# Sixteen block products in place of eighteen: a Strassen-like scheme for the second pair's up-projections

## The chip, the cores and the metric

The kernel runs on one core of one Trainium2 chip. The core has a matrix engine, TensorE (PE in the profile, its weight loads PEld), and three engines for everything between the products: VectorE (DVE), ScalarE (ACT) and GpSimd (POOL). SyncE (SP) issues the DMA transfers here, all of them on its one queue. Each engine works through its own list of instructions in order; between engines there are only semaphores. Products land in PSUM, in which the kernel uses eight banks of 128 x 512 floats; everything else lies in SBUF.

The metric is the device time of one run in microseconds. Before the change it is 773.49 us, the median of three runs (773.17 to 774.0).

## The reference, cut to what matters

```python
def _attn_ref(q, k, v, alpha):          # 4 x 8 heads, 768 steps, 48 wide
    for t in range(S):
        state = alpha[:, :, t, :, None] * state + np.einsum('bhd,bhe->bhde', k[:, :, t], v[:, :, t])
        y[:, :, t] = np.einsum('bhd,bhde->bhe', q[:, :, t], state)

def _moe_ref(x, w_in, w_out):           # 3072 x 384, w_in 384 x 2048
    h = x @ w_in
    return (h * np.cos(h)) @ w_out

def _moe2_ref(x, w1, w2, w3, w_out):    # w1, w2, w3 384 x 768, w_out 768 x 384
    h = np.maximum(np.maximum(x @ w1, x @ w2), x @ w3)
    return h @ w_out

def reference(q, k, v, alpha, moe_*, moe2_*):
    x = attn_out as 3072 rows of 384
    return _moe2_ref(_moe_ref(x, ...), ...)
```

The change concerns the three up-projections x @ w1, x @ w2 and x @ w3 of the last function.

## The kernel before

The 3072 tokens are cut into six units of 512 (HB). Features lie along the partitions, tokens along the free dimension, so a 384-wide vector is three blocks (NR) of 128. Every matrix product works on a 128 x 128 weight block and a 128 x 512 token block, and is made three times: both operands are split into a high part in TensorE's fast float format and a low remainder, and high x high, high x low and low x high are added up in PSUM. So one "block product" is three matmul instructions.

There are two stages. In the first, attention for a unit (functions turn and visit, in small matmuls) runs between the steps of the first pair of matrices: moe1, one step for each of 16 hidden blocks of 128 (NF1), 96 steps in all. A step takes three block products up (lines 665 to 667), then q, cosine and product on ACT and DVE (lines 673 to 677), the split into gh and gl (678, 679), and three block products down into the three accumulators acc (696 to 698). At the end of a unit ACT and DVE split the three accumulators into a high and a low part (lines 705, 706) and SP stores both in DRAM as x1d.

The second stage is moe2_h and moe2_o. For each unit u and each of six hidden blocks f (NF2), moe2_h takes nine block products: three weights m by three input blocks cc, lines 747 to 749, each weight into a PSUM bank of its own. ACT copies the first bank to t, DVE takes the maximum with the second (755) and the third (757), ACT and DVE split the result into h (758, 759). moe2_o multiplies h by w_out (770 to 772), ACT copies the result to y (775) and SP stores it (776). The function x2_in reads a unit's x1d back (732). The nine blocks w0h to w2l of each f are made by the function weight: the host's float64 numbers come in by DMA (line 363), ACT and DVE turn them into float32 (364, 365), ACT takes the high part (369) and POOL the remainder (373). For the second stage that happens 18 times for w1 to w3, due in steps 78 to 90 of the first stage, and six times for w_out.

The order of all of this is worked out before the program is written. Each piece of work is recorded by op with an engine, a cost, the names that it reads and writes, and a due time in steps. Program.order then plays the list through, engine by engine, taking among what is ready the piece with the smallest due time, and the instructions are written in that order; it also chooses the PSUM bank for each result (five banks ps, and the three acc). On the chip the order within an engine is fixed, and the semaphores decide when each instruction starts. A cost or a due time in the table therefore changes only the order. The flag port in op keeps a piece of POOL's work and a marked piece of DVE's apart in that plan; the written program has no semaphore for it.

Of the kernel before, what the change touches and what calls it, by code (L numbers as in the profile page):

```python
# [47 lines left out]
NWB = NW1 + 3 * NF2 + NF2  # L48
INV2PI = 1.0 / (2.0 * math.pi)
TWOPI = 2.0 * math.pi  # L50


# [4 lines left out]
LIMIT = {"h": 3, "a": 3, "t": 2, "w": 1, "r": 2, "y": 2, "r0": 2, "s0": 2}  # L57
# [184 lines left out]
def dve(n):  # L242
    return 0.07 + 0.00104 * n
# [37 lines left out]
def tile_kernel(ctx, tc, aa, qk, vv, wt, outT):  # L281
# [6 lines left out]
    x1d = dram.tile([NU, NR, P, 2, HB], F32, name="x1d")  # L288
# [17 lines left out]
    gh_b = [mp.tile([P, HB], F32R, name=f"gh{i}") for i in range(NG)]  # L306
    gl_b = [mp.tile([P, HB], F32R, name=f"gl{i}") for i in range(NG)]
    yy_b = [mp.tile([P, 2, HB], F32R, name=f"yy{i}") for i in range(2)]
# [24 lines left out]
    g_b = [ap.tile([PR, AL], F32, name=f"g{i}") for i in range(NGS)]  # L333

# [59 lines left out]
    def att0(k, p, t0):  # L394
# [7 lines left out]
        if k == 3:  # L402
            v, vk = v_b[2], ("v", 2)
            t, na = inv_b[0], "iv0"
            al_to = inv_f[0]
            gf, kg = inv_b[1][:, 0:AL], ("iv1",)
            kq_to = yy_b[1].bitcast(F32).rearrange("p a b -> p (a b)")
            kq_, kk_ = kq_to[0:PR], "yy1"
# [248 lines left out]
    def moe1(i):  # L657
# [34 lines left out]
        for c in range(NR):  # L692
# [7 lines left out]
            op("PE", 3 * mm(HB, P), omm, [("gh", gn), ("gl", gn), ("woh", f), ("wol", f)], [("acc", c)], i + 1.5)  # L700
        if f == NF1 - 1:
            for c in range(NR):
                yn = 1
                o, k = yy_b[yn], f"yy{yn}"
                op("Act", act(HB, True), lambda c=c, o=o: se.activation(o[:, 0], acc[c], AF.Copy), [("acc", c)], [(k, "h"), *((x, k) for x in ("ink", "inq") if not i // NF1)], i)
# [6 lines left out]

    def open_w2():
        s_at.close()
        wp2 = ctx.enter_context(tc.tile_pool(name="w2p", bufs=1))
        for n in "hl":
            w2t[n] = [wp2.tile([P, NF2, NR, P], F32R, name=f"w{m}{n}") for m in range(3)]

    def open_np():
        s_w1.close()  # L720
        np_ = ctx.enter_context(tc.tile_pool(name="np", bufs=1, side="right"))
        w2t["h2"] = [np_.tile([P, NF2, 2, HB], F32R, name=f"h2_{i}") for i in range(2)]
        w2t["t"] = [np_.tile([P, HB], F32, name=f"t2_{i}") for i in range(2)]
        w2t["y"] = [np_.tile([P, HB], F32, name=f"y2_{i}") for i in range(2)]
# [4 lines left out]
    def x2_in(u, t0):  # L729
        n = u % 2  # L730
        for c in range(NR):
            op("SP", HW, lambda c=c: nc.sync.dma_start(x_tile(NU + u).bitcast(F32)[:, c], x1d[u, c]),
               [("x1d", u, c)] + ([("xtA", n)] if c else []),
               [*halves(n, c), ("xp", n, c, 0), ("xp", n, c, 1)] + ([] if c else [("xtA", n)]), t0, dma(P * HB * 8))

    def moe2_h(u, f, t0):
        xn, hn, qn = u % 2, u % 2, (u * NF2 + f) % 2

        def t():
            return w2t["t"][qn]  # L740

        for m in range(3):
            k, ps = psum("a")
            for cc in range(NR):
                def hmm(cc=cc, m=m, ps=ps):
                    xt = x_tile(NU + u)
                    pe.matmul(ps, w2t["h"][m][:, f, cc], xt[:, cc, 0], start=(cc == 0), stop=False)  # L747
                    pe.matmul(ps, w2t["h"][m][:, f, cc], xt[:, cc, 1], start=False, stop=False)  # L748
                    pe.matmul(ps, w2t["l"][m][:, f, cc], xt[:, cc, 0], start=False, stop=(cc == NR - 1))  # L749

                op("PE", 3 * mm2(HB, P), hmm, [*halves(xn, cc), ("xtA", xn), ("w2h", m, f), ("w2l", m, f)], [k], t0 + 0.3 * m)
            if m == 0:
# [237 lines left out]
```

## Time and profile before

| | |
|---|---|
| Median of three runs | 773.49 us (773.17 to 774.0) |
| Span of the profiled execution | 772.1 us |
| PE busy | 762.7 us (99%), 5863 matmuls |
| DVE, ACT, POOL busy | 431.2 us (56%), 348.7 us (45%), 126.0 us (16%) |
| TensorE clock granted | 1.00 of full speed throughout |
| DMA | 72.21 MB, mean 94 GB/s |

The median of the runs is 1.4 us above the span of the profiled execution: the runs are timed from outside the program's first and last instruction. PE's matmuls overlap, since each starts before the one ahead of it has ended, so a busy PE row says that PE never waits, not that it does more in a microsecond than it can. For the other engines a row gives the time from an instruction's start to its end; two instructions that do not depend on each other may overlap by about a tenth of a microsecond. The window rows give busy microseconds of each engine in a stretch. An instruction's line in the profile is its line in the kernel before.

### The profile page before, as it was taken

Reading aid. Unit: us, or ns where it says so; the run is one execution under the profiler, and the core shown is the slowest. Engines: PE = TensorE matmul, PEld = TensorE weight load, DVE = VectorE, ACT = ScalarE, POOL = GpSimd, SP = SyncE. Lnnn points to the kernel's source line nnn. Section 1 sums busy time; section 2 is a strip of 40 time slices with the busy share of each in tenths; the row PEclk is TensorE's granted clock in tenths of the full one; section 3 lists DMA queues with packets and bytes.
Section 4 is the critical chain, followed back from the end, with each engine's and each line's share of the span. In section 5 each row is a group of like instructions: output and inputs, shape, how many; then the busy total and the mean of one; then the engine's idle time right before and its main releaser. Section 6 shows DMA issues by size and latency. Waiting matters only on the chain.

```text
span 772.1 us, 14185 instructions
## 1 busy us (share of the span) xinstructions
PE 762.7 (99%) x5863; PEld 626.8 (81%) x5863; DVE 431.2 (56%) x720; ACT 348.7 (45%) x669; POOL 126.0 (16%) x133
## 2 busy tenths in 40 slices
PE   8999999999999999999999999999999999999998
PEld 6677788888888888888888888888888888888886
DVE  8899998687856776765557654432221312213121
ACT  5788756455555655465568754411121211111121
POOL 5655431120310221110023301100000000000000
PEclk9999999999999999999999999999999999999999
DMA  9777633232312231121027504220020200200001
GB/s 342 261 234 237 187 114 108 59 105 80 118 55 60 92 116 47 45 94 36 8 82 271 167 20 139 88 81 28 14 96 28 82 27 14 96 25 4 22 19 42
DMA packets 27232, 72.21 MB, mean 94 GB/s; under 512 B 3392, under 2 KB 6464, under 8 KB 27168
## 3 DMA queue, kind: packets, MB, share of 16 engines
q1 hardware_dynamic: 27168, 71.31, 27.7%
q8 instruction: 46, 0.75, 0.4%
q14 instruction: 18, 0.15, 0.1%
HBM read 55.17 MB, written 14.16 MB: 90 GB/s over the span
## 4 chain that ended last, share of the span: by engine, by line
PE 88%; DVE 1%; ACT 1%; issue 0%; DVEq 0%; ACTq 0%
PE ps L749 10%; PE ps L748 10%; PE ps L747 9%; PE acc L696 8%; PE acc L698 8%; PE ps L665 8%; PE acc L697 8%; PE ps L667 7%; PE ps L666 7%; PE ps L771 3%; PE ps L772 3%; PE ps L770 3%; PE ps L563 1%; PE ps L581 1%; PE ps L588 1%; PE ps L537 1%
## 5 line engine op out<-in xcount | busy, mean ns | idle before, releaser
L665 PE MATMUL ps<-xt,wih 128*128 128x512 f32 x288 | 115.1, 400 | 0.4 <-ACT woh L369 0.4
L696 PE MATMUL acc<-gh,woh 128*128 128x512 f32 x288 | 114.0, 396 | 0.2 <-ACT gh L686 0.2
L698 PE MATMUL acc<-gl,woh 128*128 128x512 f32 x288 | 112.5, 391 | 0.4 <-DVE gl L691 0.4
L666 PE MATMUL ps<-xt,wih 128*128 128x512 f32 x288 | 112.3, 390 | 0.4 <-DVE xt L501 0.4
L667 PE MATMUL ps<-xt,wil 128*128 128x512 f32 x288 | 112.4, 390 | 0.0
L697 PE MATMUL acc<-gh,wol 128*128 128x512 f32 x288 | 112.2, 390 | 0.0
L674 DVE SCALAR_TENSOR_TENSOR q<-q,ps 128x512 f32<-128x512 int32 x96 | 65.4, 681 | 48.4 <-ACT q L673 48.2
L757 DVE TENSOR_TENSOR ps<-t,ps 128x512 f32<-128x512 f32 x36 | 25.1, 696 | 106.7 <-PE ps L749 106.7
L673 ACT ACTIVATE q<-ps 128x512 int32<-128x512 f32 x96 | 57.2, 595 | 57.5 <-PE ps L667 55.8
L675 ACT ACTIVATE q<-q 128x512 f32<-128x512 f32 x96 | 60.5, 631 | 43.4 <-DVE q L674 42.6
L679 DVE TENSOR_TENSOR gl<-q,gh 128x512 fp32r<-128x512 f32 x80 | 57.8, 724 | 32.9 <-ACT gh L678 30.4
L758 ACT ACTIVATE h<-ps 128x512 fp32r<-128x512 f32 x36 | 21.6, 600 | 113.4 <-DVE ps L757 113.4
L677 DVE TENSOR_TENSOR q<-q,ps 128x512 f32<-128x512 f32 x80 | 54.7, 684 | 27.5 <-ACT q L675 26.5
L678 ACT ACTIVATE gh<-q 128x512 fp32r<-128x512 f32 x80 | 50.2, 629 | 35.1 <-DVE q L677 31.9
L698 PEld LDWEIGHTS acc<-gl,woh 128*128 128x128 f32 x288 | 54.0, 188 | 13.0 <-DVE gl L691 1.3
L755 DVE TENSOR_TENSOR t<-t,ps 128x512 f32<-128x512 f32 x36 | 24.8, 688 | 71.3 <-PE ps L749 71.2
L665 PEld LDWEIGHTS ps<-xt,wih 128*128 128x128 f32 x288 | 54.1, 188 | 12.2 <-ACT woh L369 0.8
L696 PEld LDWEIGHTS acc<-gh,woh 128*128 128x128 f32 x288 | 54.0, 188 | 11.9 <-ACT gh L686 0.6
L667 PEld LDWEIGHTS ps<-xt,wil 128*128 128x128 f32 x288 | 54.1, 188 | 11.8 <-POOL wil L373 0.4
L666 PEld LDWEIGHTS ps<-xt,wih 128*128 128x128 f32 x288 | 54.1, 188 | 11.4 <-DVE xt L501 0.8
L697 PEld LDWEIGHTS acc<-gh,wol 128*128 128x128 f32 x288 | 54.1, 188 | 10.6
L775 ACT ACTIVATE y<-ps 128x512 f32<-128x512 f32 x18 | 10.8, 600 | 93.2 <-PE ps L772 93.2
(147 smaller groups left out, 1452.4 us busy)
## 6 DMA issues: line engine op xcount, KB each, us to landing
raw<-in_wt SPq DMA_DIRECT2D x56, 384.0 KB, 3.9
kq<-in_qk SPq DMA_DIRECT2D x23, 512.0 KB, 4.2
x1d<-yy SPq DMA_DIRECT2D x18, 512.0 KB, 2.7
xt<-x1d SPq DMA_DIRECT2D x18, 512.0 KB, 4.7
al<-in_aa SPq DMA_DIRECT2D x23, 261.0 KB, 2.8
outT<-y SPq DMA_DIRECT2D x18, 256.0 KB, 2.0
v<-in_vv SPq DMA_DIRECT2D x23, 192.0 KB, 4.6
xt<-yy SPq DMA_DIRECT2D x30, 64.0 KB, 3.3
```

The lines of the kernel that those rows point to most:

```text
L665: pe.matmul(ps, wi["h"][:, f, cc], xt[:, cc, 0], start=(cc == 0), stop=False)
L666: pe.matmul(ps, wi["h"][:, f, cc], xt[:, cc, 1], start=False, stop=False)
L667: pe.matmul(ps, wi["l"][:, f, cc], xt[:, cc, 0], start=False, stop=(cc == NR - 1))
L674: op("DVE", dve(HB), lambda: ve.scalar_tensor_tensor(q, q.bitcast(I32), -TWOPI, ps, ALU.mult, ALU.add), [hk], [qk], m)
L675: op("Act", act(HB), lambda: se.activation(q, q, AF.Sin, bias=0.5 * math.pi), (), [qk], m)
L679: op("DVE", dve(HB), lambda: ve.tensor_tensor(gl, q, gh.bitcast(F32), ALU.subtract), [qk, ("gh", gn)], [("gl", gn)], m, port=True)
L696: pe.matmul(acc[c], oh, gh, start=(f == 0), stop=False)
L697: pe.matmul(acc[c], ol, gh, start=False, stop=False)
L698: pe.matmul(acc[c], oh, gl, start=False, stop=(f == NF1 - 1))
L747: pe.matmul(ps, w2t["h"][m][:, f, cc], xt[:, cc, 0], start=(cc == 0), stop=False)
L748: pe.matmul(ps, w2t["h"][m][:, f, cc], xt[:, cc, 1], start=False, stop=False)
L749: pe.matmul(ps, w2t["l"][m][:, f, cc], xt[:, cc, 0], start=False, stop=(cc == NR - 1))
```

## The change

For one hidden block f and two units the kernel before computes 3 weights x 2 units x 3 input blocks = 18 block products. The changed kernel computes the same six results with 16, by a scheme of Strassen's kind: some of the products take a sum or difference of token blocks and a sum or difference of weight blocks, and the results are put together from the products by additions. There are 12 forms of token blocks for each pair of units (A_FORMS) and 16 forms of weight blocks for each f (B_FORMS). The work on one f for one pair of units is called a cell; there are 3 pairs x 6 f = 18 cells.

- **b_prep** makes the 16 weight forms, for three f at a time (a group g, two groups), during the first stage, from step 22 on and 2.6 steps apart for each of 18 weight blocks. A block is loaded and made into float32 as before (ACT, DVE), POOL makes the sums (comb), ACT and POOL split each form (split), and SP stores it in DRAM as bfd.
- **b_load** reads the 16 forms of a cell back, in two halves of 8 forms (1 MB each), into one of two buffers bs_0 and bs_1. The second buffer lies where the first stage's weights were.
- The end of a unit stores the plain accumulator (x1r, a copy by ACT) in place of a high and a low part. **a_prep** reads six such blocks for a pair, makes seven sums on POOL and splits the 12 forms on ACT and DVE: for the first pair in steps 79 to 95, for the others around the down-projections of the pair before.
- **cell** makes the 16 products, five copies of products to SBUF by ACT, one sum by POOL, and the differences and maxima on DVE; finish adds the last part in PSUM and splits h.
- **down** is moe2_o for one unit of a pair, now in one piece behind the pair's six cells; it was spread between the up-projections of the next unit.

gh and gl become the two halves of one tile gg, and the kernel is built with dynamic_dma_scratch_size=1024, which leaves more SBUF for tiles.

```diff
 
-NWB = NW1 + 3 * NF2 + NF2
+NG2 = 2
+NB2 = 9 * NG2
+WO2 = NW1 + NB2
...
+B_ORDER = ((0, 2), (1, 2), (0, 1), (0, 0), (1, 0), (2, 0), (2, 1), (2, 2), (1, 1))
+B_FORMS = ("14", "g1", "22", "21", "6", "23", "13", "8", "10", "15", "7", "11", "2", "9", "12", "32")
+A_FORMS = ("S14", "S1", "a22", "T", "P", "Q", "a11", "a21", "S10", "a13", "a23", "S7")
+NBW, NAS, NH2 = 7, 12, 12
+B_START, B_STEP = 22, 2.6
...
-                op("DVE", dve(HB), lambda c=c, o=o: ve.tensor_tensor(
-                    o[:, 1], acc[c], o.bitcast(F32)[:, 0], ALU.subtract), [("acc", c), (k, "h")], [(k, "l")], i)
-                op("SP", HW, lambda c=c, o=o: nc.sync.dma_start(x1d[u, c], o.bitcast(F32)), [(k, "h"), (k, "l")], [("x1d", u, c)], i, dma(P * HB * 8))
+                op("SP", HW, lambda c=c, o=o: nc.sync.dma_start(x1r[u, c], o), [k], [("x1r", u, c)], i, dma(P * HB * 4))
...
+    def b_prep(g, first, gate):
...
+        def load(j, buf):
...
+                op("Act", act(WB) + 0.1, lambda: se.activation(upper, head, AF.Copy), [rk], [("top", 0)], t)
+                op("DVE", dve(WB), lambda: ve.scalar_tensor_tensor(o.bitcast(U32), x, 13, top, ALU.logical_shift_right, ALU.bitwise_or), [("top", 0), rk], [("bw", buf)], t, port=True)
...
+        def comb(to, x, y, sub=True):
+            op("Pool", pool(WB), lambda: ge.tensor_tensor(bw_b[to], bw_b[x], bw_b[y], ALU.subtract if sub else ALU.add), [("bw", x), ("bw", y)], [("bw", to)], n[0] + 0.1)
+
+        def split(name, buf):
...
+            op("Act", act(WB), lambda: se.activation(st[:, :, 0], x, AF.Copy), [("bw", buf)], [("bs", m, 0)], n[0] + 0.2)
+            op("Pool", pool(WB), lambda: ge.tensor_tensor(st[:, :, 1], x, st.bitcast(F32)[:, :, 0], ALU.subtract), [("bw", buf), ("bs", m, 0)], [("bs", m, 1)], n[0] + 0.2)
+            op("SP", HW, lambda: nc.sync.dma_start(bfd[3 * g:3 * g + 3, :, i].rearrange("f p h n -> p f h n"), st.bitcast(F32)),
+               [("bs", m, 0), ("bs", m, 1)], [("bfd", g, i)], n[0] + 0.3, dma(P * WB * 8))
...
+    def a_prep(p, t0, dt, gate=None):
...
+    def b_load(ci, t0):
+        f, x = ci % NF2, ci % 2
+        for h in range(2):
+            hs = slice(NBF // 2 * h, NBF // 2 * (h + 1))
+            op("SP", HW, lambda hs=hs: nc.sync.dma_start(w2t[f"bs{x}"].bitcast(F32)[:, hs], bfd[f, :, hs]),
+               [("bfd", f // 3, i) for i in range(hs.start, hs.stop)] + ["w2", *(["np"] if x else [])], [("Bs", x, h)], t0 + 1.33 * h, dma(P * NBF * P * 4))
...
+    def cell(p, f, t0):
...
+                pe.matmul(bank, bt[:, i, 0], at[:, 0], start=start, stop=False, skip_group_check=skip)
+                pe.matmul(bank, bt[:, i, 0], at[:, 1], start=False, stop=False, skip_group_check=skip)
+                pe.matmul(bank, bt[:, i, 1], at[:, 0], start=False, stop=stop, skip_group_check=skip)
...
+        product(d21, k21, "S14", "14", True, True)
+        copy("14", d21, k21)
+        product(d23, k23, "S1", "g1", True, True)
+        copy("1", d23, k23)
+        both("u", "14", "1", ALU.add)
+        k12, d12 = psum("m")
+        product(d12, k12, "a22", "22", True, True)
+        copy("22", d12, k12)
+        k11, d11 = psum("m")
+        product(d11, k11, "T", "21", True, True)
+        copy("12", d11, k11)
+        product(d12, k12, "P", "6", False, True)
+        join("s1", d12, k12, "u", ALU.subtract, True)
+        k13, d13 = psum("m")
+        product(d13, k13, "Q", "23", True, True)
+        copy("16", d13, k13)
+        product(d11, k11, "a11", "13", False, True)
+        join("s1", d11, k11, "s1", ALU.max)
+        product(d21, k21, "a21", "8", False, False)
+        product(d21, k21, "S10", "10", False, True)
+        join("s2", d21, k21, "12", ALU.subtract)
+        both("s2", "s2", "22", ALU.max)
+        product(d13, k13, "a13", "15", False, True)
+        join("s1", d13, k13, "s1", ALU.max)
+        r1k, r1 = psum("m")
+        product(r1, r1k, "a11", "7", True, True)
+        product(r1, r1k, "a13", "11", False, True)
+        finish(0, r1, r1k, "s1")
+        product(d23, k23, "a23", "2", False, False)
+        product(d23, k23, "S7", "9", False, True)
+        join("v", d23, k23, "16", ALU.subtract)
+        both("s2", "s2", "v", ALU.max)
+        r2k, r2 = psum("m")
+        product(r2, r2k, "a21", "12", True, True)
+        product(r2, r2k, "a23", "32", False, True)
+        finish(1, r2, r2k, "s2")
...
+        for g in range(NG2):
+            b_prep(g, first, lambda j: B_START + B_STEP * j)
...
+        a_prep(0, NS - 17, 1.1, NS - 17)
+        b_load(0, NS - 6)
...
+        b_load(1, NS + 0.5)
...
+                cell(p, f, t)
...
+                    b_load(n, t + 1.33)
...
+                a_prep(p + 1, t - CB, 0.2)
```

Where the order changes, three places show how. The rows name line, operation and tiles (result, arrow, operands, with the numbers of their buffers); the lines of the changed kernel are its own.

The first is TensorE in the up-projections of the second stage, before: xt6 holds a unit's tokens, w1h to w2l are high and low parts of weights, ps4 and ps1 two PSUM banks.

```order
L747 MATMUL ps4_103<-xt6_4328,w1h_4229 128x512
L748 MATMUL ps4_103<-xt6_4328,w1h_4229 128x512
L749 MATMUL ps4_103<-xt6_4328,w1l_4232 128x512
L747 MATMUL ps1_100<-xt6_4328,w2h_4230 128x512
L748 MATMUL ps1_100<-xt6_4328,w2h_4230 128x512
L749 MATMUL ps1_100<-xt6_4328,w2l_4233 128x512
```

In the changed kernel, the third to the sixth product of a cell: as2 to as5 are token forms, bs_1 is a buffer of weight forms.

```order
L907 MATMUL ps1_99<-as2_4400,bs_1_4978 128x512
L908 MATMUL ps1_99<-as2_4400,bs_1_4978 128x512
L909 MATMUL ps1_99<-as2_4400,bs_1_4978 128x512
L907 MATMUL ps3_101<-as3_4401,bs_1_4978 128x512
L908 MATMUL ps3_101<-as3_4401,bs_1_4978 128x512
L909 MATMUL ps3_101<-as3_4401,bs_1_4978 128x512
L907 MATMUL ps4_102<-as5_4403,bs_1_4978 128x512
L908 MATMUL ps4_102<-as5_4403,bs_1_4978 128x512
L909 MATMUL ps4_102<-as5_4403,bs_1_4978 128x512
L907 MATMUL ps1_99<-as4_4402,bs_1_4978 128x512
L908 MATMUL ps1_99<-as4_4402,bs_1_4978 128x512
L909 MATMUL ps1_99<-as4_4402,bs_1_4978 128x512
```

A bank of before is filled by nine matmuls in a row and read afterwards; in a cell the sixth product adds to ps1, which the third has filled and which ACT copies in between, with two products of other banks behind the third.

The second is ACT in the second stage, before: t2 is the first of the three maxima's operands, h2 the high part of the result.

```order
L753 ACTIVATE t2_0_4845<-ps4_103 128x512
L758 ACTIVATE h2_1_4844<-ps0_99 128x512
L753 ACTIVATE t2_1_4846<-ps2_101 128x512
L758 ACTIVATE h2_1_4844<-ps4_103 128x512
L753 ACTIVATE t2_0_4845<-ps1_100 128x512
```

And one cell of the changed kernel, with the high part h2_5 of the cell before it: q and xf hold the copied products.

```order
L915 ACTIVATE q_83<-acc0_95 128x512
L915 ACTIVATE q_83<-acc1_96 128x512
L932 ACTIVATE h2_5_4984<-ps0_98 128x512
L915 ACTIVATE q_83<-ps1_99 128x512
L915 ACTIVATE xf_4931<-ps3_101 128x512
L915 ACTIVATE xf_4931<-ps4_102 128x512
L932 ACTIVATE h2_6_4985<-ps2_100 128x512
```

The copy of ps1, for which the sixth product waits, stands behind the last result of the cell before.

The third is POOL in the first stage, before: kq holds keys and queries of the attention, g and al its decay factors, d a state.

```order
L527 TENSOR_TENSOR kq0_104<-kq0_104,al0_124 112x512
L642 TENSOR_TENSOR d0_112<-s3_118,g2_129 112x192
L524 TENSOR_TENSOR kq1_105<-kq1_105,g1_128 112x512
L527 TENSOR_TENSOR kq1_105<-kq1_105,al1_125 112x512
L642 TENSOR_TENSOR d0_112<-s0_115,g0_127 112x192
```

At the same place of the changed kernel (its attention buffers have other numbers), bw are weight blocks and sums of them, bs their split forms:

```order
L539 TENSOR_TENSOR kq0_103<-kq0_103,al0_123 112x512
L786 TENSOR_TENSOR bw0_129<-bw0_129,bw2_131 128x384
L794 TENSOR_TENSOR bs0_136<-bw2_131,bs0_136 128x3x128
L794 TENSOR_TENSOR bs1_137<-bw0_129,bs1_137 128x3x128
L654 TENSOR_TENSOR d0_111<-s3_117,g2_128 112x192
L786 TENSOR_TENSOR bw4_133<-bw3_132,bw2_131 128x384
L786 TENSOR_TENSOR bw3_132<-bw3_132,bw1_130 128x384
L786 TENSOR_TENSOR bw2_131<-bw2_131,bw1_130 128x384
L794 TENSOR_TENSOR bs0_136<-bw4_133,bs0_136 128x3x128
L794 TENSOR_TENSOR bs1_137<-bw3_132,bs1_137 128x3x128
L536 TENSOR_TENSOR kq1_104<-kq1_104,g1_127 112x512
L539 TENSOR_TENSOR kq1_104<-kq1_104,al1_124 112x512
```

Between two multiplications of the attention there now stand eight pieces of the weight forms, and the d of before is among them.

## Rows read from the trace of the kernel before

**Rows 1.** Windows: stretch, length, busy us and instructions by engine, clock, DMA.
```profile
80.00:100.00 20.00, 19.39 (x240) 15.16 (x232) 18.76 (x36) 13.94 (x30) 9.38 (x11) 1.00 0.52 160
100.00:134.00 34.00, 34.00 (x455) 28.03 (x453) 30.56 (x53) 20.50 (x41) 7.68 (x7) 1.00 0.39 125
134.00:354.00 220.00, 220.00 (x2429) 181.95 (x2421) 158.25 (x266) 121.01 (x233) 38.84 (x36) 1.00 0.24 79
354.00:480.00 126.00, 126.00 (x748) 104.03 (x739) 74.66 (x120) 76.21 (x141) 22.03 (x22) 1.00 0.32 102
480.00:768.00 288.00, 288.00 (x1272) 238.36 (x1270) 77.32 (x112) 56.73 (x96) 4.48 (x5) 1.00 0.13 46
```

**Rows 2.** Timeline of PE (start us, us, engine, line, operation, tiles).
```profile
470.26 0.39 PE L747 MATMUL ps<-xt,w0h 128*128 128x512 f32 x1
...
480.46 0.39 PE L747 MATMUL ps<-xt,w0h 128*128 128x512 f32 x1
```

**Rows 3.** Groups by line: count, busy us, mean ns, idle before.
```profile
L747 PE MATMUL ps<-xt,w0h 128*128 128x512 f32 x108 | 42.0, 389 | 0.0
```

**Rows 4.** Windows of line 696 alone (PE busy and count).
```profile
0.00:134.00 134.00, 23.05 (x57) 10.70 (x57) 1.00 0.65 214
134.00:354.00 220.00, 55.57 (x141) 26.46 (x141) 1.00 0.24 79
```

**Rows 5.** Groups by line, other engines.
```profile
L364 ACT ACTIVATE top<-raw 128x384 f16<-128x384 bf16 x56 | 35.6, 640 | 2.3 <-DMA raw<-in_wt 1.9
L524 POOL TENSOR_TENSOR kq<-kq,g 112x512 f32<-112x512 f32 x20 | 26.7, 1333 | 58.3 <-DMA kq<-in_qk 29.0 <-DVE g L521 12.4 <-DVE inv L523 7.5
...
L365 DVE SCALAR_TENSOR_TENSOR raw<-raw,top 128x384 uint32<-128x384 uint32 x40 | 25.4, 635 | 3.4 <-ACT top L364 2.0 <-issue 1.2
...
L373 POOL TENSOR_TENSOR wil<-raw,wih 128x384 fp32r<-128x384 f32 x16 | 16.8, 1052 | 20.2 <-ACT wih L369 17.7 <-DVE inv L431 1.8 <-POOL kq L649 0.5
...
L369 ACT ACTIVATE w1h<-raw 128x384 fp32r<-128x384 f32 x6 | 3.3, 550 | 2.0 <-DVE raw L365 2.0
```

**Rows 6.** Line 677 by itself: ns min/median/max, first and last start.
```profile
L677 DVE TENSOR_TENSOR q<-q,ps x80: 652/689/691, 111.3 to 472.5; 128x512 f32<-128x512 f32 x80
```

**Rows 7.** Line 679 by itself, in the same form.
```profile
L679 DVE TENSOR_TENSOR gl<-q,gh x80: 649/692/1646, 113.8 to 473.9; 128x512 fp32r<-128x512 f32 x80
```

**Rows 8.** Timeline, 400 to 404 us, DVE and POOL.
```profile
400.06 0.56 DVE L365 SCALAR_TENSOR_TENSOR raw<-raw,top 128x384 uint32<-128x384 uint32 x1 [0.37 <-ACT top L364]
...
402.18 1.04 POOL L373 TENSOR_TENSOR w0l<-raw,w0h 128x384 fp32r<-128x384 f32 x1 [4.25 <-ACT w0h L369]
...
402.73 0.90 DVE L365 SCALAR_TENSOR_TENSOR raw<-raw,top 128x384 uint32<-128x384 uint32 x1 [0.36 <-ACT top L364]
```

**Rows 9.** Timeline, 84.8 to 87.2 us, ACT, PE and DVE.
```profile
84.84 0.59 ACT L686 ACTIVATE gh<-ps 128x512 fp32r<-128x512 f32 x1
...
85.31 0.61 ACT L673 ACTIVATE q<-ps 128x512 int32<-128x512 f32 x1
...
85.48 0.50 PE L696 MATMUL acc<-gh,woh 128*128 128x512 f32 x1 [0.18 <-ACT gh L686]
...
85.82 0.40 PE L697 MATMUL acc<-gh,wol 128*128 128x512 f32 x1
85.91 0.68 DVE L691 TENSOR_TENSOR gl<-ps,gh 128x512 fp32r<-128x512 f32 x1
...
86.51 0.68 DVE L674 SCALAR_TENSOR_TENSOR q<-q,ps 128x512 f32<-128x512 int32 x1
```

**Rows 10.** Timeline at 560 us: issues on SP's queue.
```profile
560.21 1.28 SPq L732 DMA_DIRECT2D xt<-x1d  x3
```

**Rows 11.** DMA issues by line: KB each, median us to landing.
```profile
xt<-x1d SPq DMA_DIRECT2D x18, 512.0 KB, 4.7
```

**Rows 12.** Timeline of POOL at 251 us.
```profile
251.37 1.20 POOL L527 TENSOR_TENSOR kq<-kq,al 112x512 f32<-112x512 f32 x1
```

**Rows 13.** Timeline of PE at 276 us.
```profile
276.70 0.69 PE L563 MATMUL ps<-kq 48*64 48x64 f32 x32
```

More of the change, by code (lines that the diff above doesn't have):

```diff
@@ L56 @@
 NBANK = 5
[L57 removed]
+LIMIT = {"h": 3, "m": 4, "t": 2, "w": 1, "r": 2, "y": 2, "r0": 2, "s0": 2}
 GLE1, GLQ = 0, 16
@@ L333, in tile_kernel @@
     g_b = [ap.tile([PR, AL], F32, name=f"g{i}") for i in range(NGS)]
+    bw_b = [ap.tile([P, WB], F32, name=f"bw{i}") for i in range(NBW)]
+    bs_b = [ap.tile([P, 3, 2, P], F32R, name=f"bs{i}") for i in range(2)]
     chosen = {}
@@ new lines, in a_prep, with due, step, comb @@
+    def a_prep(p, t0, dt, gate=None):
+        ar = lambda i: w2t["ar"][i]
+        R = {f"a{i + 1}{k + 1}": 3 * i + k for i in range(2) for k in range(NR)}
+        m = [0]
+        def due():
+            return t0 + dt * m[0]
+        def step():
+            return [("step", int(gate + dt * m[0]))] if gate else []
+        for x in ("a12", "a22", "a11", "a13", "a23", "a21"):
+            i = R[x]
+            op("SP", HW, lambda i=i: nc.sync.dma_start(ar(i), x1r[2 * p + i // 3, i % 3]), [("x1r", 2 * p + i // 3, i % 3), "w2"], [("ar", i)], t0 - 2, dma(P * HB * 4), tiled=True)
+        def comb(to, x, y, sub=False):
+            op("Pool", pool(HB), lambda: ge.tensor_tensor(ar(to), ar(x), ar(y), ALU.subtract if sub else ALU.add), [("ar", x), ("ar", y), *step()], [("ar", to)], due())
+        def split(name, i):
+            n = A_FORMS.index(name)
+            o = lambda: a_slot(n)
+            hk, lk = ("as", n, 0), ("as", n, 1)
+            extra = x_freed(0) if n == 9 and not p else []
+            need = [("xtA", 0)] if n in (10, 11) and not p else []
+            op("Act", act(HB), lambda: se.activation(o()[:, 0], ar(i), AF.Copy), [("ar", i), "w2", *need, *step()], [hk, *extra], due())
+            op("DVE", dve(HB), lambda: ve.tensor_tensor(o()[:, 1], ar(i), o().bitcast(F32)[:, 0], ALU.subtract), [("ar", i), hk], [lk], due(), port=True)
+            m[0] += 1
+        comb(6, R["a12"], R["a22"])
+        comb(7, R["a11"], R["a12"])
+        split("Q", 7)
+        comb(R["a12"], R["a12"], R["a13"], True)
+        split("P", 6)
+        comb(7, R["a12"], R["a22"])
+        split("S14", 7)
+        comb(6, 6, R["a11"])
+        split("S1", 6)
+        split("a22", R["a22"])
+        split("T", R["a12"])
+        comb(7, 7, R["a23"], True)
+        split("a11", R["a11"])
+        split("a21", R["a21"])
+        split("S10", 7)
+        comb(6, 6, R["a21"])
+        split("a13", R["a13"])
+        split("a23", R["a23"])
+        split("S7", 6)
@@ L882, in build @@
-        for c in range(NR):
-            moe2_o(NU - 1, c, NS + 2 + NB * NU + c)
+            weight(WO2 + f, lambda f=f: w2t["oh"][:, f], lambda f=f: w2t["ol"][:, f],
+                   ("w2oh", f), ("w2ol", f), NS + 8 + f, ["np"])
+        CB = 16 / 6
+        PB = NF2 * CB + 6
+        for p in range(NU // 2):
+            t0 = NS + 2 + PB * p
+            for f in range(NF2):
+                t = t0 + CB * f
+                cell(p, f, t)
+                n = NF2 * p + f + 2
+                if n < NF2 * NU // 2:
+                    b_load(n, t + 1.33)
+            t = t0 + CB * NF2
+            if p + 1 < NU // 2:
+                a_prep(p + 1, t - CB, 0.2)
+            for i in range(2):
+                for c in range(NR):
+                    down(p, i, c, t + 3 * i + c)
@@ L969 @@
     w1 = _np.stack([blocks(inputs["moe_w_in"], rows), outs(inputs["moe_w_out"])], 1).reshape(-1, P, WB)
-    w2 = _np.stack([blocks(inputs["moe2_" + n]) for n in ("w1", "w2", "w3")], 1).reshape(-1, P, WB)
+    ws = [_np.asarray(inputs["moe2_" + n]) for n in ("w1", "w2", "w3")]
+    w2 = _np.stack([ws[m][k * P:(k + 1) * P, g * WB:(g + 1) * WB] for g in range(NG2) for k, m in B_ORDER])
     wt = _np.ascontiguousarray(_np.concatenate([w1, w2, outs(inputs["moe2_w_out"])]))
```

212 lines of the change are left out of this document (138 added, 74 removed).

## The prediction

> **What bounds the kernel now.** I read the windows first, then the stretch in which the changed code runs. From 100 us on PE is busy in every microsecond of every window: 34.00 of 34.00, 220.00 of 220.00, 126.00 of 126.00, 288.00 of 288.00; between 80 and 100 us it lacks 0.61 [rows 1]. The clock column is 1.00, so all of this is at the upper level, 2.4 GHz. In the second stage, from 480 us, DVE is busy 77.3 of 288 us, ACT 56.7, POOL 4.5, and DMA 0.13 of its time: PE alone sets the end, and the others have three quarters of their time free. Then comes the price of one matmul. A group's row gives 389 ns for it [rows 3], but matmuls overlap. From the one at 470.26 to the one 45 places later at 480.46 [rows 2] it is 10.20 / 45 = 0.2267 us from start to start, and that is what one more or one less is worth.
>
> **The matmuls removed.** A hidden block of two units took 18 block products, 54 matmuls, and takes 16, 48. The trace has 108 matmuls for each of nine kinds (three weights, three lines; one of the nine is in [rows 3]), 972 in all; 18 cells x 48 are 864. 108 x 0.2267 = 24.5 us less on the engine that sets the end. The 324 down matmuls stay, in blocks of 108 behind each pair. Whether the 24.5 us are kept depends on what PE has to wait for, so each addition is held against PE's time.
>
> **Weight forms, in the first stage.** Line 696 has 57 matmuls before 134 us and 141 from there to 354 us [rows 4]; three make a step, so this stretch holds steps 19 to 65. b_prep, from step 22 on with its first load gated on step 19, lies in it almost whole. Before, the 18 weight blocks of w1 to w3 were made later, around 400 us [rows 8]. Added here: 18 x 0.64 and 32 x 0.55 us on ACT, 18 x 0.635 on DVE, 24 sums and 32 remainders at about 1.05 on POOL [rows 5]. That is 29, 11 and 59 us, which makes ACT 150, DVE 170 and POOL 98 of 220 us. None of these is full.
>
> DVE and POOL disturb each other, though. The same instruction of line 365 took 0.56 us at 400.06 with POOL idle and 0.90 at 402.73 beside POOL's of 402.18 [rows 8]. Line 679, with both operands in SBUF, ranges to 1.646 us over a median of 0.692 [rows 7]; line 677, with one operand in PSUM, stays between 0.652 and 0.691 [rows 6]. If each of POOL's 56 pieces costs DVE 0.34 us, DVE is at 189 of 220 us, 86%. From 100 to 134 us it was at 30.56 of 34, 90%, and PE waited for nothing; from 80 to 100 us it was at 94% and PE lacked 0.61 us. The bounds are therefore 0 and 0.61 x 11 = 6.7 us; less than nothing is excluded, since PE has no idle time here to give back. I take 0.5, near the row with the like load. What hides the work is that a step gives PE four microseconds and that its chain on ACT and DVE runs ahead of PE; where that cover is gone, each late gl holds PE, and all of PE's queue behind it.
>
> The Trainium skill has a rule that speaks against this edit ("SBUF — State Buffer", section "Who interferes with whom"): a DVE instruction with two SBUF inputs contends with a GpSimd instruction that reads SBUF, for one port pair that is locked for a whole instruction. This trace agrees: line 679 suffers and line 677 does not. By that rule alone each of the 56 pieces can block DVE for its whole length, and the sum would be that of the second rival below.
>
> SP's queue gets 32 stores that wait for POOL's remainders, with loads for the attention behind them. Those have room: POOL's product of 251.37 [rows 12] is used by PE's matmuls from 276.70 on [rows 13], 24 us later. Cost 0; once the room is gone, a visit of the attention would wait on PE.
>
> **Token forms.** A pair costs 12 copies on ACT, 12 subtractions on DVE and 7 sums on POOL, at about 0.60, 0.69 and 1.33 us [rows 9, 7, 5]: 7, 8 and 9 us. The first pair's fall in steps 79 to 95, from which the 18 weight blocks have gone; DVE was at 74.7 of 126 us there with them [rows 1]. The others fall beside 108 down matmuls, 24.5 us. Cost 0. The 18 subtractions at the units' ends leave DVE, for which PE did not wait: gain 0.
>
> **The cell.** Sixteen products take 16 x 0.680 = 10.88 us. DVE has 11 pieces of 0.69, 7.6 us; ACT 7 of 0.60, 4.2; POOL one of 1.33. What matters is the chain. Product k (from 0) starts 0.68 k after the cell and can be read at 0.68 k + 0.84 (two pitches and 0.389); an engine is taken to start 0.04 after that, an estimate. The narrow place is the sixth product, due at 3.40, whose bank ACT has to copy first; ACT's queue ahead of that copy holds the high part of the previous cell's last result. In that cell DVE takes product 9 at 7.00 (a maximum), then the maximum in SBUF, the sum with product 11 at 8.36 to 9.05; ACT's high part ends at 9.69, DVE's low part starts at 9.72, v at 10.32, the next maximum at 11.05, the last sum at 11.77 to 12.46, which is 1.58 in the new cell. The steps of 0.60 and not 0.68 between instructions that do not depend on each other are those of DVE's two starts at 85.91 and 86.51; ACT's are 0.47 at 84.84 and 85.31 [rows 9]. ACT then copies product 1 at 1.56, the high part at 2.03, the third product at 2.50 to 3.10. With no overlap at all DVE ends at 1.87 and that copy at 3.40. PE goes on 0.16 us after ACT: gh ended at 85.43, the second matmul behind it started at 85.82, so the first went at 85.59 [rows 9]. The sixth product can thus go at 3.26, before its turn, or at 3.56, 0.16 late. The bounds are 0 and 0.16 us in each of the 15 cells that follow a cell, 0 and 2.4 us; I take 0.3, since the rows show the overlap. Next narrowest is the second product: v has read its bank at 11.01, and it is due at 11.56.
>
> **Weight forms read back.** Each cell reads 2 x 1.05 MB, of which it has 10.88 us: 193 GB/s. Three loads of 512 KB were issued within 1.28 us [rows 10] and took 4.7 us to land [rows 11], so 1.57 MB in at most 6.0 us, 262 GB/s: 8.0 us for a cell. Taken as one at a time, 0.52 MB in 4.7 us are 112 GB/s and 18.8 us for a cell. I take the first, as the rows describe loads side by side, and cost 0. The second buffer's first load can only go when the first stage's last product is done; 12 products, 8.2 us, then stand ahead of the second cell, and half a buffer needs 4.0 to 6.0.
>
> **The sum.** 772.1 - 24.5 + 0.5 + 0.3 = 748.4 us of span; the last copy and store are as before. The runs lie 1.4 us above the span, so 749.8 us for the median, 23.7 less, 3.1%.
>
> **The rivals.**
> - *The cell's chain is the longer one.* 0.16 us late in 15 cells: 749.8 - 0.3 + 2.4 = 751.9; at twice that, 754.3. For it: a slack of a tenth of a microsecond. Against it: DVE has 3 us of each cell free, so a late cell does not add up with the next.
> - *DVE and POOL lock each other in the first stage.* If each of 56 pieces costs DVE 0.95 us, the excess of the longest in [rows 7], DVE is wanted for 223 of 220 us and stops hiding; with 0.34 of each then on PE it is 749.3 + 19 = 768. It decides from about 95% of DVE in that stretch. Against it: PE's idle 0.00 at 90%.
> - *The weight forms come late (slower).* If a cell's loads take 18.8 us, PE waits 7.9 us at 16 cells, 126 us: 876. It decides from 10.88 us per cell; at 12.4 the gain is used up. For it: the landing time of one load, and one queue that issues them between other work. Against it: 262 GB/s in [rows 10, 11], and a DMA share of 0.13 in this stage.
> - *Nothing moves.* The 24.5 us come back as waits, a mixture of the first two, at 773.5. Against it: no row shows an engine that full.
>
> **How the numbers follow.** My forecast, with small waits only, 749.0 to 751.0: chance 0.72. The cell's chain, up to 754.3: 0.13. The lock, 753 to 768: 0.09. No change: 0.02. The late weight forms: 0.04. Faster by over 0.2% (1.5 us, about what a measurement of this kernel can tell from no change) holds the first three, 0.94. The range takes the forecast and the cell's chain: below it reaches to the removal without any wait, 749.0, less the 0.6 us that PE lacked at 80 to 100 us; above to 755.
>
> **What would show it.** Right: 108 matmuls fewer, no wait of PE over 0.2 us behind 100 us, a cell every 10.9 us. PE waiting for ACT at a cell's sixth product, or for DVE at its second, is the first rival; for gl between 134 and 354 us, with DVE above 95%, the second; for DMA at a cell's first or ninth product, the third, which would make the prediction wrong.

## The result and the profile after

The changed kernel took 752.26 us, median of four runs (750.11 to 754.11), against 773.48 before in the same comparison: a ratio of 0.972, interval 0.9692 to 0.9747. Five more runs of the same file gave 750.45 (749.70 to 750.74) against 774.04, 0.9695 [0.9682, 0.9709]. Forecast were 749.8 and a range of 748.4 to 755.0. Two experiments were profiled in executions well above their medians: of s2_eighteen (846.65 us) only the times are used, of s9_one_plan (758.95 us) the times and the stretch from 80 us on, where the granted clock was 1.00, and a sixth run of s9_one_plan, 921.20 us, is left out.

The windows of the changed kernel, over the same stretches as [rows 1] (length, busy us and instructions of PE, PEld, DVE, ACT, POOL, clock, DMA share, GB/s):

```profile
80.00:100.00 20.00, 19.14 (x249) 14.91 (x238) 18.84 (x35) 13.79 (x30) 9.07 (x10) 1.00 0.37 112
100.00:134.00 34.00, 34.00 (x336) 28.02 (x335) 28.33 (x47) 19.36 (x40) 9.10 (x9) 1.00 0.34 114
134.00:354.00 220.00, 220.00 (x2422) 181.68 (x2421) 160.32 (x273) 143.34 (x284) 97.14 (x91) 1.00 0.51 160
354.00:480.00 126.00, 125.74 (x853) 103.59 (x852) 73.48 (x113) 70.08 (x125) 17.08 (x15) 1.00 0.18 57
480.00:745.00 265.00, 265.00 (x1170) 218.92 (x1169) 148.35 (x225) 94.83 (x172) 45.67 (x35) 1.00 0.48 164
```

PE still has no gap in the second stage, although DVE there rose from 77 to 148 us, POOL from 4 to 46 and the DMA share from 0.13 to 0.48. The cover that the prediction counted on is there. PE's timeline has the stage's edges and the first product of two neighbouring cells, the third and the fourth:

```profile
478.40 0.39 PE L710 MATMUL acc<-gg,woh 128*128 128x512 f32 x1
...
497.66 0.39 PE L907 MATMUL acc<-as,bs 128*128 128x512 f32 x1
...
508.56 0.39 PE L907 MATMUL acc<-as,bs 128*128 128x512 f32 x1
...
745.03 0.39 PE L984 MATMUL acc<-h,wo2h 128*128 128x512 f32 x1
```

From cell to cell it is 10.90 us, and 48 pitches of [rows 2] are 10.88. Behind 478.40 no two matmuls start more than 0.24 us apart. Where PE waited at all from 80 us on (waiting line, releaser, us in total, times, longest):

```profile
PE acc L710 <- DVE gg L703: 0.4, 1, 0.4
PE ps L593 <- DVE q L689: 0.3, 1, 0.3
PE acc L708 <- ACT gg L698: 0.2, 1, 0.2
PE ps L600 <- ACT z L664: 0.2, 1, 0.2
```

Three of the four lie before 88 us, where PE already lacked 0.6 us before the change [rows 1]; that for q is at 356.5, in the attention. None is a cell's. The weight forms' groups (count, busy us, mean ns, idle before), and gl beside them, which is gg here:

```profile
L691 DVE TENSOR_TENSOR gg<-q,gg 128x512 fp32r<-128x512 f32 x80 | 59.0, 741 | 25.3 <-ACT gg L690 24.6
...
L794 POOL TENSOR_TENSOR bs<-bw,bs 128x384 fp32r<-128x384 f32 x32 | 33.6, 1056 | 27.6 <-ACT bs L793 27.5
...
L786 POOL TENSOR_TENSOR bw<-bw,bw 128x384 f32<-128x384 f32 x24 | 26.4, 1108 | 29.5 <-DVE bw L780 28.8
```

POOL's 56 pieces cost 60 us, as forecast (59). The transfers (KB each, median us from issue to landing), where the 512 KB of [rows 11] took 4.7:

```profile
bs<-bfd SPq DMA_DIRECT2D x36, 1024.0 KB, 5.1
...
bfd<-bs SPq DMA_DIRECT2D x32, 384.0 KB, 3.1
```

How the loads of 1 MB follow one another in the cells, on SP's queue (start, length, issues):

```profile
486.98 22.10 SPq L888 DMA_DIRECT2D bs<-bfd  x5
```

Five issues in 22.10 us are one each 5.4 us, half a cell. Each waits until PE has read the half buffer that it overwrites. With a median of 5.1 us the one before has landed by then: behind the first few, the loads run about one at a time.

**Where the time went.** The profiled span fell from 772.1 to 749.0, 23.1 us. The last matmul moved from 767.87 to 745.03, 22.84, where 108 x 0.2267 are 24.48, so 1.64 came back. Line for line it lies in the first stage. The down matmuls of step 15 came 0.69 later (110.12 against 109.43), before any weight form is made, and in the second profile of the same file only 0.12 later (109.55), so that part varies between executions. From step 25 to step 75 it took 236.39 us, and 236.62 in the second profile, against 235.48 before: 0.9 to 1.1 us, in the stretch of the weight forms. The last copy and store took 0.28 less. Of the 0.91 us in the first profile one visit of the attention, a block of 128 small matmuls, explains 0.48: it took 2.43 us from its first matmul's start to its last one's end, the other 13 behind 130 us took 1.95. The rest lies in shifts too short for the list of waits.

### The profile page after: what moved, and what is told of

It reads as the page before. It is cut to its first block, busy times and chain, and to the rows that moved or that the text cites. A ratio compares the mean times of both kernels' runs of the same rounds, so it can differ in the third digit from the quotient of the medians.

```text
span 749.0 us, 14516 instructions
## 1 busy us (share of the span) xinstructions
PE 739.3 (99%) x5755; PEld 606.0 (81%) x5755; DVE 500.3 (67%) x828; ACT 400.9 (54%) x773; POOL 221.6 (30%) x210
## 4 chain that ended last, share of the span: by engine, by line
PE 89%; ACT 4%; DMA 2%; DVE 2%; issue 1%; POOL 1%; SPq 0%; DVEq 0%; ACTq 0%; POOLq 0%
PE acc L708 8%; PE acc L710 8%; PE acc L709 8%; PE ps L677 8%; PE ps L679 8%; PE ps L678 8%; PE ps L908 5%; PE ps L907 5%; PE ps L909 5%; PE acc L908 3%; PE acc L907 3%; PE acc L909 3%; PE acc L983 2%; PE acc L982 2%; PE ps L983 2%; PE ps L982 2%
## 5 line engine op out<-in xcount | busy, mean ns | idle before, releaser
L708 PE MATMUL acc<-gg,woh 128*128 128x512 f32 x288 | 114.2, 396 | 0.2 <-ACT gg L698 0.2
L710 PE MATMUL acc<-gg,woh 128*128 128x512 f32 x288 | 112.8, 392 | 0.4 <-DVE gg L703 0.4
L709 PE MATMUL acc<-gg,wol 128*128 128x512 f32 x288 | 112.2, 390 | 0.0
L691 DVE TENSOR_TENSOR gg<-q,gg 128x512 fp32r<-128x512 f32 x80 | 59.0, 741 | 25.3 <-ACT gg L690 24.6
L926 POOL TENSOR_TENSOR xf<-q 128x512 f32<-128x512 f32 x18 | 23.3, 1296 | 170.3 <-ACT q L915 165.0
L690 ACT ACTIVATE gg<-q 128x512 fp32r<-128x512 f32 x80 | 50.5, 631 | 38.1 <-DVE q L689 28.6
L710 PEld LDWEIGHTS acc<-gg,woh 128*128 128x128 f32 x288 | 54.0, 188 | 13.6 <-DVE gg L703 1.3
L708 PEld LDWEIGHTS acc<-gg,woh 128*128 128x128 f32 x288 | 54.0, 188 | 12.2 <-ACT gg L698 0.7
L709 PEld LDWEIGHTS acc<-gg,wol 128*128 128x128 f32 x288 | 54.1, 188 | 10.7
L852 POOL TENSOR_TENSOR ar<-ar,ar 128x512 f32<-128x512 f32 x21 | 30.1, 1444 | 84.5 <-DVE as L861 48.3
L920 DVE TENSOR_TENSOR xf<-xf,ps 128x512 f32<-128x512 f32 x18 | 12.4, 687 | 58.5 <-PE ps L909 51.8
```

Of the source, the lines that this page charges most:

```text
L691: op("DVE", dve(HB), lambda: ve.tensor_tensor(gl, q, gh.bitcast(F32), ALU.subtract), [qk, ("gh", gn)], [("gl", gn)], m, port=True)
L708: pe.matmul(acc[c], oh, gh, start=(f == 0), stop=False)
L709: pe.matmul(acc[c], ol, gh, start=False, stop=False)
L710: pe.matmul(acc[c], oh, gl, start=False, stop=(f == NF1 - 1))
```

## The experiments

**s1_same and s2_eighteen: the price of the matmuls.** The first is the changed kernel itself, the base of its group. In the second two products of each cell are made twice:

```diff
+            product(r1, r1k, "a11", "7", True, True)
             product(r1, r1k, "a11", "7", True, True)
...
+            product(r2, r2k, "a21", "12", True, True)
             product(r2, r2k, "a21", "12", True, True)
-        CB = 16 / 6
+        CB = 18 / 6
```

> The changed kernel as it is, for its spread. Its four runs lay between 750.1 and 754.1 us, while those of before stay within 0.9 us. Theory 1 (PE alone is the bound; the second stage waits for nothing; what is left over 748.4 us of span is lost in the first stage): the profile again shows no PE wait in a cell, the second stage takes 1188 x 0.2267 = 269.3 us, and a slower execution is longer ahead of the last step of the first stage. Rival A (the forms read back come late in some executions): a slower execution has PE waits for DMA at a cell's first or ninth product. Rival B (the cell's chain): waits for ACT or DVE at the sixth or second product.

> Each cell makes two of its products twice (the second one overwrites the first), so 18 in place of 16, with everything else of the scheme kept. Theory 1: 108 matmuls x 0.2267 = 24.5 us more than the changed kernel, so 775 to 777 us, 1 to 3 above the kernel before; that is then the whole price of the additions. Rival A or B (the cells hide waits that the extra products fill): clearly less than 24.5 us, 15 to 22, and a smaller spread.

Measured: 750.45 and 774.96 (ratio 1.0011 [1.0002, 1.002] to before). The 108 matmuls cost 24.5 us, as worked out from one pitch. What is left for all the rest of the change is 0.9 us (0.2 to 1.5), just under theory 1's 1 to 3: with 18 products it takes nearly the time of the kernel before. In the profile of s1_same, too, PE waited in no cell.

**s3_pool_twice and s4_no_read.** Each remainder is made twice on POOL; or the forms are read back for the first pair only, which leaves 24 loads of 1 MB out, so the second and third pairs compute with the wrong blocks of weights. The edits here and below are shortened.

```diff
# s3_pool_twice
+            for _ in range(2):
                 op("Pool", pool(WB), lambda: ge.tensor_tensor(st[:, :, 1], x, ...
# s4_no_read
-                if n < NF2 * NU // 2:
+                if n < NF2:
                     b_load(n, t + 1.33)
```

> POOL makes each remainder of a weight form twice: 32 more pieces of about 1.05 us in the first stage, 88 in place of 56. Theory 1: POOL and DVE have room, within 1 us of the changed kernel. Rival C (DVE and POOL lock each other and PE feels it): 32 x 0.34 = 11 us if all of it reaches PE, at least 2 to 4 us, with PE waits for gl between 134 and 354 us and DVE busy over 170 of 220 us.

> The weight forms are read back for the first pair only; the 12 cells of the other two pairs use what lies in the buffers (that leaves out 24 loads of 1 MB). Theory 1: 0 to 0.5 us less than the changed kernel, the spread as before. Rival A: the spread goes, all runs near the fastest of the changed kernel, the median 2 us lower.

Measured: 751.69 (751.38 to 751.96), 1.24 us more for 32 us more of POOL, and 751.73 (751.06 to 753.55). Without 24 loads nothing was gained, and PE waits for no DMA in the lists, so reading back costs nothing. But s4_no_read, whose first stage is unchanged, was expected to be lower and lies 1.28 us up. So the 1.24 us of s3_pool_twice, just above theory 1's 1 us, are not told from how such kernels differ. PE had no wait for gl in s3_pool_twice; it waited twice, 2.0 us in all, for the bank that q x ps (line 689) frees.

The trace of s4_no_read shows one mechanism that lengthens the first stage. DVE, POOL and the PE row that waits, in order of time:

```profile
295.82 1.27 POOL L794 TENSOR_TENSOR bs<-bw,bs 128x384 fp32r<-128x384 f32 x1 [1.62 <-ACT bs L793]
296.14 2.06 DVE L533 TENSOR_TENSOR_SCAN g<-al,one 112x520 f32<-112x520 f32 x1
...
297.26 1.72 POOL L794 TENSOR_TENSOR bs<-bw,bs 128x384 fp32r<-128x384 f32 x1 [0.17 <-ACT bs L793]
298.12 0.66 DVE L689 TENSOR_TENSOR q<-q,ps 128x512 f32<-128x512 f32 x1
...
298.92 0.69 PE L575 MATMUL ps<-kq 48*64 48x64 f32 x32 [0.76 <-DVE q L689]
```

The scan's median is 1.23 us and a remainder's 1.02; overlapping, they took 2.06 and 1.72. Behind the scan stands the product q x ps, the last reader of a PSUM bank, and the attention's matmuls want that bank: PE waits 0.76 us. It is not the only one. The changed kernel's own wait at 356.5 us is for the same product, yet DVE's pieces in the four us ahead of it took their usual 0.56 and 0.69 us, and s4_no_read's longest wait, 1.00 us at 357.0, has none stretched close ahead of it either. What makes those late stays open.

**s5 to s8: less POOL, more stores, another engine, another spacing.**

```diff
# s5_no_pool: 22 sums and 30 remainders are left out
+            if not g and to == 5 or not g and (to, x) == (4, 3):
                 op("Pool", ..., comb)
+            if first[0] <= 2:
                 op("Pool", ..., remainder)
# s6_store_twice
+            for _ in range(2):
                 op("SP", HW, lambda: nc.sync.dma_start(bfd[...], st...
# s7_remainders_dve
-            op("Pool", pool(WB), lambda: ge.tensor_tensor(st[:, :, 1], ...
+            op("DVE", dve(WB), lambda: ve.tensor_tensor(st[:, :, 1], ... port=True)
# s8_spread
-B_START, B_STEP = 22, 2.6
+B_START, B_STEP = 22, 3.1
```

> Leaves out 22 of the 24 sums and 30 of the 32 remainders on POOL, so the stored low halves and most sums are stale; loads, ACT's high halves, stores and read-back stay. Theory A (POOL's pieces beside DVE's delay the DVE instruction that frees a PSUM bank, and PE's attention matmuls wait for it): the 0.9 to 2.4 us that the changed kernel's first stage lost between steps 25 and 75 are gone; down matmuls of step 25 to step 75 take 235.5 us as in the kernel before, every attention visit 1.97 us behind 130 us, time about 749.3, 1 us under the changed kernel. Theory B (the traffic of stores and loads or ACT's added copies are the cost): unchanged, 236.4 to 238 us for the fifty steps, time 750.5.

> Each of the 32 stores of 384 KB is issued twice, so 12.6 MB more in the first stage and SP's queue longer; results unchanged. Theory A (POOL against DVE): nothing, 750.5, fifty steps 236.4 to 237. Theory B (DMA traffic of the added forms slows the first stage): the loss of 0.9 to 2.4 us grows by as much again, time 751.5 to 753.

> The 32 remainders go from POOL to DVE, 32 x about 0.55 us, so DVE goes from 160 to 178 of 220 us between 134 and 354 us and POOL loses 34 us. Theory A (the overlap of the two engines is the cost): fewer stretched scans, loss of the fifty steps down from 0.9-2.4 to 0.4-1.0 us, time 749.7 to 750.2. Rival (DVE's own queue is the cost, however it is filled): DVE's added work delays the same bank by as much or more, fifty steps 236.5 to 239, time 750.5 to 753.

> The weight forms' steps are 3.1 steps apart in place of 2.6 and end at step 75 in place of 66; same instructions. Theory A: the attention ends near step 65, so about a sixth of POOL's pieces leave the stretch where DVE is full and the rest lie thinner; loss down by a sixth to a third, 750.0 to 750.4. Theory B (traffic): spread traffic costs the same, 750.5. If the last forms come too late for the second stage, PE waits at its first cells and the time rises by several us.

Measured, with the fifty steps from each trace: s5 749.50 (748.69 to 751.67), 235.40 us; s6 748.99 (748.87 to 751.29), 235.86; s7 749.43 (748.39 to 749.92), 236.02; s8 750.89 (749.77 to 751.62), 236.75. The fifty steps run from the down matmuls of step 25 to those of step 75. In the trace theory A holds for s5: without most of POOL's pieces the fifty steps take what they took before. Theory B's growth with s6 did not come. Theory A's smaller loss with s8 did not come either: 1.3 us over 235.48, where the changed kernel has 0.9 and 1.1. But the times lie within 1.9 us of each other, and s6, which adds work, is the lowest. Each of the four edits makes the planner lay out another order of DVE's instructions, and the planner also runs over a set whose order changes with the build. Nor is the order all: s4_no_read has the changed kernel's order on DVE and POOL, and its fifty steps took 237.91 us. So the last group holds the order.

**s9 to s12: the order held.** The planner's one loop over a set is made an ordered one; the other three kernels then have the instructions of s9_one_plan in the same order on every engine, with only the named pieces shorter or doubled inside their own operation, so that the planner does not know of it.

```diff
# s9_one_plan, and all of the group
-        for k in {*reads, *writes}:
+        for k in dict.fromkeys((*reads, *writes)):
# s10_pool_short: 52 pieces on 8 or 3 x 8 columns
+            ge.tensor_tensor(bw_b[to][:, 0:w], ...); ge.tensor_tensor(st[:, :, 1, 0:w], ...
# s11_pool_more
-            lambda: ge.tensor_tensor(st[:, :, 1], ...)
+            lambda: [ge.tensor_tensor(st[:, :, 1], ...) for _ in range(2)]
# s12_store_more
-            lambda: nc.sync.dma_start(bfd[...], ...)
+            lambda: [nc.sync.dma_start(bfd[...], ...) for _ in range(2)]
```

> The changed kernel with the planner's one unordered loop (over the keys of an operation) made an ordered one, so that every build has the same order of instructions; nothing else. It is the base of the next three, which have exactly its order on PE, DVE, ACT and SP or POOL. Theory A (POOL beside DVE, then a bank that comes free late) and theory B (traffic) both give the changed kernel's 750.5 within the effect of another order, 749 to 752, with fifty steps (down matmuls of step 25 to 75) of 236 to 237.5 us against 235.5 before.

> Same order of all instructions as s9_one_plan; 52 of POOL's 56 pieces are cut from 384 columns to 8 or 3 x 8, which leaves out most of the sums and low halves. Theory A: the fifty steps fall to 235.5 us and the visits of the attention all take 1.97 us, so 0.5 to 2 us less than s9_one_plan. Theory B, or a rival in which the order of instructions alone (DVE's and ACT's added work) sets the loss: no difference to s9_one_plan.

> Same order as s9_one_plan; each of the 32 remainders is made twice in a row on POOL, 34 us more of POOL in the stretch of the attention. Theory A: the fifty steps 0.5 to 1.5 us longer than in s9_one_plan, with more visits above 1.97 us. Theory B or order alone: no difference.

> Same order as s9_one_plan; each of the 32 stores of 384 KB is issued twice in a row, 12.6 MB more in the first stage. Theory A: no difference to s9_one_plan, below 0.3 us. Theory B (traffic): the loss over 235.5 us for the fifty steps grows by half or more.

Measured: s9 749.86 (four of five runs 749.70 to 750.02), s10 749.59 (748.63 to 753.42), s11 765.44 (765.21 to 765.74), s12 784.35 (781.52 to 788.21). The fifty steps took 238.65, 235.77, 251.52 and 269.34 us. The last two kernels missed what was expected of them by an order of size.

In s10 PE is full in both windows of the weight forms, and all 14 visits behind 130 us take 1.95 us:

```profile
134.00:354.00 220.00, 220.00 (x2424) 181.58 (x2423) 160.41 (x275) 142.87 (x282) 55.09 (x90) 1.00 0.50 158
354.00:480.00 126.00, 126.00 (x855) 104.18 (x854) 74.78 (x115) 70.34 (x125) 16.70 (x14) 1.00 0.19 59
```

PE's waits in the profile of s9, with the same order and the whole pieces:

```profile
PE acc L710 <- DVE gg L691: 0.8, 1, 0.8
PE ps L593 <- DVE q L689: 0.6, 1, 0.6
...
PE acc L708 <- ACT gg L690: 0.4, 1, 0.4
```

So in the traces shorter pieces of POOL take 2.9 us off the fifty steps, as theory A has it, and one of the waits was for gl. In the times they do not: s10's median is 0.27 us under s9's, which the runs don't tell from nothing, and the profiled execution of s9 was not a usual one. What POOL's pieces cost in a usual execution is therefore not settled beyond about a microsecond.

In s11 the same 32 pieces that went with 1.24 us in s3_pool_twice cost 15.6. First PE's waits, then line 691 alone (ns min, median, max):

```profile
PE acc L710 <- DVE gg L691: 5.6, 7, 1.2
PE acc L708 <- ACT yy L717: 1.4, 2, 1.1
PE ps L593 <- DVE q L689: 1.2, 1, 1.2
PE ps L549 <- POOL kq L536: 1.1, 1, 1.1
```

```profile
L691 DVE TENSOR_TENSOR gg<-q,gg x80: 660/693/2239, 113.5 to 489.6; 128x512 fp32r<-128x512 f32 x80
```

PE waits most for gl, where the prediction's second rival had placed it. Between 134 and 420 us gl's mean is 925 ns, 712 in s1_same and 750 in s3_pool_twice. The planner tells the two kernels apart: it marks POOL's pieces and DVE's instructions with two SBUF operands as users of one port (port_free in its ready()), and lets none start before the last has ended. Told of the pieces (s3) it steps around them; not told (s11), more of them collide. How much of the 15.6 us is the collision, and how much that a fixed order holds everything behind a longer piece, was not separated.

In s12 it is not the traffic: from 134 to 354 us it moved 184 GB/s at a DMA share of 0.56, and s6_store_twice 209 at 0.64 without loss. Waits of SP, of ACT and of PE, in this order:

```profile
SPq L795 <- DMA bfd<-bs: 98.7, 32, 6.6
SPq L795 <- POOL bs L794: 39.5, 14, 8.0
```

```profile
ACT top L779 <- DMA raw<-in_wt: 23.4, 7, 5.9
...
ACT bs L793 <- DMA bfd<-bs: 13.9, 9, 2.5
```

```profile
PE acc L708 <- ACT gg L690: 12.0, 4, 4.7
PE acc L710 <- DVE gg L691: 4.4, 4, 2.4
```

The second store goes to the place of the first and waits until that has landed, 32 times 3.1 us, at the head of SP's queue. The loads behind it come late, ACT stands for them and for the store's buffer, and gh behind ACT's wait comes late for PE. The longest case, rows of SP, ACT and PE:

```profile
311.69 9.49 SPq L795 DMA_DIRECT2D bfd<-bs  x4
...
322.38 0.49 SPq L778 DMA_DIRECT2D raw<-in_wt  x1
```

```profile
327.55 0.63 ACT L779 ACTIVATE top<-raw 128x384 f16<-128x384 bf16 x1 [5.19 <-DMA raw<-in_wt]
328.05 0.60 ACT L690 ACTIVATE gg<-q 128x512 fp32r<-128x512 f32 x1
```

```profile
328.71 0.80 PE L708 MATMUL acc<-gg,woh 128*128 128x512 f32 x1 [4.72 <-ACT gg L690]
```

A part is the clock. About the end of this wait, and of two more of 3.2 and 2.6 us, the granted clock fell to its lower level, 1.2 GHz: it was 0.51 from 328.3 to 331.8 us, and again in the 3.5 us from 365.8 and from 393.1. By estimate (three times 3.5 us at half the clock) that is up to 5 of the 34 us. In s6_store_twice second stores waited too (31.0 us, 19 times), but the planner knew of them and put them elsewhere: no wait of ACT for a store came of it, and no loss.

## Why the prediction was right

- **Matmuls removed, -24.5.** Right: from the pitch of one row, and s2_eighteen gave 24.5 as well, between medians of runs that spread by 1 to 2 us.
- **Weight forms, +0.5.** The cover held, the size was about twice that: 0.9 and 1.1 us in the two profiles of the changed kernel, 0.4 to 1.3 with other orders (s6 to s8), but 2.4 in s4_no_read and 3.2 in the profile of s9. Engine loads came out at 143, 160 and 97 of 220 us against 150, 170 and 98. The place was wrong: PE waited hardly for gl (0.8 us in s9) but, at the attention's visits or a step's first up product, for the bank that q x ps frees. The prediction's own sign, no wait over 0.2 us behind 100 us, failed by the 0.3 us at 356.5. And 0.34 us for each of POOL's pieces was far too much. DVE took 160.3 us where s5_no_pool, almost without the pieces, took 158.6 with four instructions more, by estimate 0.03 to 0.07 us each. The likely reason is the planner's order, which keeps most of the two apart. The prediction read the lock from rows before and missed what stood in the code against it. The rule of the Trainium skill that it cites ("SBUF — State Buffer", section "Who interferes with whom") agrees with s11_pool_more, where nothing kept the added pieces apart and gl's mean rose to 925 ns.
- **SP's queue, 0.** Right in the changed kernel; from 134 to 420 us SP stands there for 70.0 us, in 24 waits, for POOL's remainders, without harm. The warning was right as well, but it named the attention's loads; in s12_store_more, ACT's loads and buffers came first.
- **Token forms, 0.** Right: 125.74 of 126 us between 354 and 480, and the 0.26 is the wait at 356.5, ahead of the first pair's forms.
- **The cell, +0.3.** Nothing was lost: cells 10.88 to 10.93 us apart. The narrow place at the sixth product held. The first rival, up to 4.8 us, fell.
- **Forms read back, 0.** Right, but not for the reason given. The prediction took the loads to run side by side, at 262 GB/s; in most cells they ran about one at a time, as its slower rival had it. That was enough because 1 MB landed in 5.1 us, where the rival took 4.7 us for each 512 KB: two loads are 10.2 us, of the 10.88 of a cell and not 8.0. s4_no_read gained nothing by leaving them out.
- **From span to time.** 1.4 us were taken; the profiled run lay 1.8 above its span (750.78 - 749.0).
- **The range** held both medians and all nine runs. The first median, 752.26, lies outside the forecast of 749.0 to 751.0, in the part of the range that was given to the cell's chain, of which no trace shows anything: that it was held is luck. The second, 750.45, lies in the forecast. What stays open is why runs of the same file range from 749.7 to 754.1. Part lies ahead of step 15 (0.12 and 0.69 us late in two profiles). Part is the clock: its mean was 0.995 in the run of 754.11 us, and in the first 25 us of a profile it was 0.93 (s6), 0.86 (s10) and 0.73 (s9), in runs 2.3, 3.8 and 9.1 us above their medians. In the run of 753.74 it was 1.000, so that is not all. Nor is the spread shown to be the change's: the kernel before stayed within 0.9 us in its first four runs, but ranged over 2.1, 3.5 and 2.8 us in the three later comparisons.

No version beats the changed kernel by more than it varies: s7_remainders_dve has 0.9669 [0.9652, 0.9687] against 0.9695 [0.9682, 0.9709] of another comparison.

## What to carry to other kernels

Where one engine is full and starts an instruction at a steady pitch, fewer of its instructions are worth count times pitch, and the work is to show for every addition what hides it. Whether two engines collide is a question to the order as much as to the hardware: the same 32 pieces went with 1.2 us planned for and 15.6 us unplanned. An edit that makes a planner lay out a new order can't be read for effects of a microsecond; hold the order, and change the size of one piece. Even then a trace of one execution can show what the other runs' times do not.

## What was not expected of the hardware

In a collision the rows of both sides stretch: a scan of 1.23 us to 2.06 and POOL's 1.02 to 1.72 (s4_no_read). Together the two remainders and the scan took 3.16 us there, from 295.82 to 298.98, and alone they would be 3.27 (1.02 + 1.23 + 1.02, an estimate): about as if one ran after the other. In s11_pool_more gl's longest was 2.24 us, over a median of 0.69; in the changed kernel it is 1.82. With POOL's pieces at 24 elements a partition one still took 0.24 us, so 1/16 of the work was not 1/16 of the time. And a load of 1 MB landed in 5.1 us by itself, little more than the 4.7 of 512 KB in [rows 11], of which three were under way at once.
